# Attention and gated mixing in one kernel: first loads in halves, batch 0 in other banks, the last pair by subtiles, five chunks of q norms off TensorE, and a new set of planning numbers

## The chip, the cores and the metric

The kernel runs on one core of a Trainium2 chip. The metric is the device time of one execution in microseconds (us). Runs come as a median with their lowest and highest. A ratio is the mean time of one kernel's fast runs over the mean of the other's fast runs of the same rounds, with a 95% interval, so it is not quite the ratio of the medians quoted beside it. A run is called slow when it took over 1.5% longer than the fastest of its kernel. In the profiles PE is TensorE (PEld: its weight loads), DVE VectorE, ACT ScalarE, POOL GpSimd and SP SyncE; a q after the name marks the engine's issuing of transfers. The granted clock is TensorE's clock as a share of full speed.

## The reference, cut to what matters

```python
# q, k, v: 4 x 6336 x 256, float32
qn = q / (norm(q, axis=1) + 1e-06);  kn = k / (norm(k, axis=1) + 1e-06)
a = softmax(kn.transpose(0, 2, 1) @ qn / tau)       # 4 x 256 x 256
x = (v @ a).reshape(25344, 256)
H = maximum(x @ w_h, 0);  T = sigmoid(x @ w_t + b_t)
out = T * H + (1 - T) * x                           # float32
```

## The kernel before

Each batch has two stages. Stage one accumulates k.q and the squares over 50 subtiles of rows, 48 of 128 and two of 96 ("statistics"). A chain follows: norms, a broadcast of them (`cqb`), two exponentials, their transposes (`eps`), and weights folded with the attention matrix (`mr`). Stage two takes the rows of v in 25 pairs of subtiles: three products (`t`, `h`, `d`), a tanh and a relu on ScalarE, and two operations on VectorE, of which the second writes the result `o`. Four pairs fill one chunk of 1 MB, which SyncE stores to memory. A batch has six chunks and a tail pair. Stage one of batch b+1 is mixed into stage two of batch b.

A planner inside the program orders all of this when the program is built: it takes tasks with priorities, durations and buffers, and writes out one fixed order for each engine. So a changed duration or priority can move instructions anywhere.

Result chunks live in a ring of buffers, and stores are held back, so that they do not compete with the loads too early:

```python
O_BUFS = 7
LAG = 5
...
    def hold(b, j):                       # SyncE reads one row of a result
        nc.sync.dma_start(out=held_row, in_=og[(b, j)][0:1, 0, :])

    def plan_holds():
        for x, b, j in chunk_stores:      # x: the store of chunk b * NJ + j
            n = b * NJ + j + LAG
            y, g = begun.get(n, (None, 1e9))
            ...                           # late chunks are not held
            x.key = g + 1.6
            plan.add("SP", g + 1.5, 0.1, 0, [y], lambda n=n: hold(n // NJ, n % NJ), size=1024)
```

The tiny read `held_row` stands ahead of the store in SyncE's order, and it needs the first result of chunk n+LAG. So the store of chunk n is issued once chunk n+5 has begun, and its buffer is needed when chunk n+7 begins.

Places that the change touches:

```python
    for j in range(1, NJ - 1):            # first loads, in order of issue
        plan_load("q", 0, j);  plan_load("k", 0, j)
    ...                                   # tail; chunk 5 in quarters
    plan_load("q", 1, 0);  plan_load("k", 1, 0)
    ...                                   # w_h, w_t, then the bias
    plan_load("v", 0, 0)
...
    sg_t[b] = [new(f"sg{c}", [P, 512], f32, f"sg{c}_{b}") for c in range(2)]
...
    gs = act(copy_g, 0.58, 0.7, [dk], drop=[(first, "sg0"), (first, "sg1")])
```

## Time and profile before

| | before |
|---|---|
| median of 3 runs | 273.9 us (273.01 to 275.34) |
| span of the profiled run, its mean granted clock | 271.6 us, 0.985 |
| first product / last `d` group / last store issued | 48.47 / 263.51 / 265.88 us |

The list of DMA issues (size, then median us from issue to landing) says what it needs:

```profile
out_dram<-o SPq DMA_DIRECT2D x23, 1024.0 KB, 9.1
```

19.6 us for a transfer of about 9: nothing waits, and in the costliest groups VectorE's results have only 1.9 us of idle time before all 96 of them.

### The profile page before, as it was taken

How to read it: one execution, taken by the hardware profiler on the slowest of the kernel's cores; microseconds unless marked ns; L12 is line 12 of the kernel's file. 1: busy time of each engine (PE TensorE's matmuls, PEld its weight loads, DVE VectorE, ACT ScalarE, POOL GpSimd, SP SyncE). 2: the span in 40 equal slices, each digit the busy share in tenths (PEclk: the TensorE clock that was granted, in tenths of full speed). 3: DMA queues.
4: the chain of work that ended last, by engine and by line, in shares of the span. 5: the costliest groups of instructions: out<-in, count | busy, mean ns of one | idle time of the engine just before them, and what ended most of it. 6: DMA issues, size and time to landing. Idle time of an engine off the chain costs nothing.

```text
span 271.6 us, 6265 instructions
## 1 busy us (share of the span) xinstructions
PE 247.0 (91%) x2447; PEld 218.6 (80%) x2447; DVE 177.8 (65%) x366; ACT 191.5 (71%) x361; POOL 115.3 (42%) x153
## 2 busy tenths in 40 slices
PE   0697859999999999999999999999999999999980
PEld 0596757798999988999999888999998778878870
DVE  1000033658757897778777886767766888999991
ACT  1000034868969888889897888887875989988970
POOL 7221668596691095566928167775002110000000
PEclk9999997999999999999999999999999999999996
DMA  6999999999999999999999999999999999999996
GB/s 109 212 216 214 199 208 214 214 213 215 215 211 215 212 214 219 284 233 279 289 277 255 257 289 233 270 255 275 268 288 272 330 320 316 203 345 279 283 417 241
DMA packets 28430, 68.29 MB, mean 251 GB/s; under 512 B 13168, under 2 KB 15856, under 8 KB 25456
## 3 DMA queue, kind: packets, MB, share of 16 engines
q0 software_dynamic: 13184, 39.20, 73.6%
q1 hardware_dynamic: 15216, 28.69, 30.5%
q8 instruction: 19, 0.31, 0.4%
q14 instruction: 11, 0.09, 0.1%
HBM read 78.38 MB, written 25.95 MB: 384 GB/s over the span
## 4 chain that ended last, share of the span: by engine, by line
PE 76%; DMA 13%; DVE 4%; ACT 2%; issue 2%; POOL 1%; DVEq 0%; ACTq 0%; POOLq 0%
PE d L778 15%; PE h L778 15%; PE t L778 15%; DMA k<-in_k_dram 13%; PE sg L432 12%; PE sg L433 6%; PE vtps L738 6%; PE sg L435 2%; PE ah L667 1%; DVE pp L839 1%; PE t L809 1%; DVE o L858 1%; ACT d L818 1%; ACT uu L832 1%; PE eps L657 1%
## 5 line engine op out<-in xcount | busy, mean ns | idle before, releaser
L778 PEld LDWEIGHTS <-vtsb 128*128 128x128 f16 (+1 forms) x948 | 90.0, 99 | 13.4 <-issue 3.0
L432 PE MATMUL sg<-q,k 128*128 128x256 f16 x384 | 85.7, 278 | 15.2 <-DMA k<-in_k_dram 15.1
L839 DVE SCALAR_TENSOR_TENSOR pp<-uu,d 128x512 f32<-128x512 f32 (+1 forms) x100 | 67.7, 683 | 25.0 <-PE d L778 14.8
L433 PE MATMUL sg<-k 128*128 128x128 f16 x384 | 78.8, 224 | 0.0
L832 ACT ACTIVATE uu<-t 128x512 f32<-128x512 f32 (+1 forms) x100 | 59.5, 599 | 18.6 <-PE t L778 17.2
L858 DVE SCALAR_TENSOR_TENSOR o<-h,pp 128x512 f32<-128x512 f32 x96 | 65.3, 687 | 1.9
L818 ACT ACTIVATE d<-h 128x512 f32<-128x512 f32 (+1 forms) x100 | 57.8, 585 | 5.3 <-PE h L778 4.0
L432 PEld LDWEIGHTS <-k 128*128 128x128 f16 x384 | 38.5, 100 | 18.6 <-DMA k<-in_k_dram 15.9
L450 ACT ACTIVATE sq<-q 128x1024 f32<-128x1024 f16 x24 | 25.0, 1052 | 36.0 <-DMA q<-in_q_dram 36.0
L778 PE MATMUL t<-mr,vtsb 128*128 128x256 f16 x316 | 47.2, 272 | 0.4 <-ACT t L513 0.3
L778 PE MATMUL d<-mr,vtsb 128*128 128x256 f16 x316 | 46.5, 272 | 0.3 <-ACT d L818 0.2
L778 PE MATMUL h<-mr,vtsb 128*128 128x256 f16 x316 | 46.5, 272 | 0.3 <-DVE ri L635 0.3
L435 PE MATMUL sg<-q 128*128 128x128 f16 x192 | 42.8, 223 | 0.0
L433 PEld LDWEIGHTS <-k 128*128 128x128 f16 x384 | 38.3, 100 | 1.5 <-issue 0.3
L456 POOL TENSOR_TENSOR sq<-sq,sq 128x1024 f32<-128x1024 f32 x12 | 28.4, 2368 | 22.3 <-ACT sq L450 22.3
L513 ACT COPY t<-bias_all 128x512 f32<-128x512 f32 (+1 forms) x61 | 36.1, 592 | 1.3
L738 PE MATMUL vtps<-ident,v 128*128 128x128 f32 x144 | 27.9, 275 | 0.5 <-DVE vtsb L515 0.5
L549 DVE SCALAR_TENSOR_TENSOR junk<-sg,ident 128x128 f32<-128x128 f32 x16 | 4.6, 288 | 36.1 <-PE sg L435 35.5
L778 PEld LDWEIGHTS <-vT 128*128 128x128 f16 x240 | 23.4, 98 | 4.5 <-issue 0.5
L311 POOL DMA_DIRECT2D v<-in_v_dram x24 | 13.3, 555 | 31.1 <-PE vtps L738 21.9
L515 DVE COPY vtsb<-vtps 128x256 f32<-128x256 f32 (+2 forms) x42 | 17.6, 419 | 10.0 <-PE vtps L738 9.9
L311 POOL DMA_DIRECT2D q<-in_q_dram x27 | 15.1, 558 | 16.0 <-DMA q<-in_q_dram 8.9
(77 smaller groups left out, 252.1 us busy)
## 6 DMA issues: line engine op xcount, KB each, us to landing
out_dram<-o SPq DMA_DIRECT2D x23, 1024.0 KB, 9.1
v<-in_v_dram POOLq DMA_DIRECT2D x24, 512.0 KB, 18.1
q<-in_q_dram POOLq DMA_DIRECT2D x23, 512.0 KB, 16.7
k<-in_k_dram POOLq DMA_DIRECT2D x23, 512.0 KB, 17.6
out_dram<-o SPq DMA_DIRECT2D x2, 512.0 KB, 6.3
out_dram<-ot SPq DMA_DIRECT2D x4, 192.0 KB, 5.8
q<-in_q_dram POOLq DMA_DIRECT2D x4, 128.0 KB, 8.6
k<-in_k_dram POOLq DMA_DIRECT2D x4, 128.0 KB, 6.6
```

The lines of the kernel that those rows point to most:

```text
L311: nc.gpsimd.dma_start(out=t[:, s : s + n, :], in_=main_rows(src)[:, j * CH + s : j * CH + s + n, :])
L432: nc.tensor.matmul(sg[c][:, 0:C], kc, qa, start=first, stop=False)
L433: nc.tensor.matmul(sg[c][:, C : C + P], kc, kc, start=False, stop=False)
L435: nc.tensor.matmul(sg[c][:, C + P : C + 2 * P], qa[:, cs], qa[:, cs], start=False, stop=last)
L456: add(out=sq, in0=sq, in1=other)
L513: nc.scalar.copy(out=out, in_=in_)
L738: nc.tensor.transpose(ps[:, u, 0:nr], v.bitcast(f32), ident0[0:nr, 0:nr])
L778: nc.tensor.matmul(out[0:nr, u, :], vt[u][kt][:, 0:nr], mr[kt][:, col * C : (col + 1) * C], **flags(u, kt))
L818: nc.scalar.activation(out=d[0:nr, :, :], in_=ps_t["h", b, i][0:nr, :, :], func=Act.Relu, scale=0.5)
L832: nc.scalar.activation(out=uu[0:nr, :, :], in_=ps_t.pop(("t", b, i))[0:nr, :, :], func=Act.Tanh, scale=-0.5)
L839: nc.vector.scalar_tensor_tensor(out=pp[0:nr, :, :], in0=el.pop(("uu", b, i))[0:nr, :, :], scalar=1.0, in1=ps_t.pop(("d", b, i))[0:nr, :, ...
L858: nc.vector.scalar_tensor_tensor(out=ot, in0=ps_t.pop(("h", b, i))[0:nr, :, :], scalar=0.0, in1=el.pop(("pp", b, i))[0:nr, :, :], op0=AluO ...
```

## The change

Its intent: begin the products of batch 0 earlier, shorten the end, take q norms of a fifth chunk off TensorE, and retune the planner's numbers for the new shape. The diff, cut to its core:

```diff
-LAG = 5
-UNTIL = 65
-AHEAD = 15
-BY_DMA = 1
-MOVE = 150e3
-APART = 4
-V_AHEAD = -2
+LAG = 6
+UNTIL = 61
+AHEAD = 20
+BY_DMA = 3
+MOVE = 165e3
+APART = 5
+V_AHEAD = 0
 PRIO = {  # ... twelve pairs of priorities, all other values
-ENDS = [17.5, 46, 64.5]
+ENDS = [24.5, 46, 68.5]
 ...
-    for j in range(1, NJ - 1):
+    b_ld = [ ... load_b(u) ... ]          # the bias now right after chunk 0
+    for j in range(1, NJ - 2):
 ...
+    for n, j in ((2, NJ - 2), (1, NJ), (4, NJ - 1)):
+        for part in range(n):
+            plan_load("q", 0, j, n, part); plan_load("k", 0, j, n, part)
-    plan_load("q", 1, 0)
-    plan_load("k", 1, 0)
+    plan_load("q", 1, 0, 2, 0)            # halves
+    plan_load("k", 1, 0, 2, 0)
     w_ld = [ ... ]
-    plan_load("v", 0, 0)
+    plan_load("v", 0, 0, 2, 0)
+    plan_load("q", 1, 0, 2, 1); plan_load("k", 1, 0, 2, 1); plan_load("v", 0, 0, 2, 1)
 ...
+    def sg_tag(b, c):
+        return f"sg{c}" if b else "h"     # batch 0 in the banks of h
 ...
+            halves = [slice(0, 1), slice(1, 2)] if g == NP * B - 1 else [slice(0, 2)]
 ...                                       # product and result once per half
```

The cut leaves out `HEAD` and `TAIL` (6 to 4, 63 to 67), a fixed order of the relus with each tanh behind its relu, the transposes of batch 0's exponentials in a bank of `h`, and two finer rules of the planner.

## The prediction

> **What bounds the kernel now.** I read the views from coarse to fine: the page's busy shares and its slices, then the stretches, then every instruction around the end of the first batch's statistics and around the end of the kernel. The page first.
>
> ```profile
> PE 247.0 (91%) x2447; PEld 218.6 (80%) x2447; DVE 177.8 (65%) x366; ACT 191.5 (71%) x361; POOL 115.3 (42%) x153
> ...
> PE   0697859999999999999999999999999999999980
> ...
> GB/s 109 212 216 214 199 208 214 214 213 215 215 211 215 212 214 219 284 233 279 289 277 255 257 289 233 270 255 275 268 288 272 330 320 316 203 345 279 283 417 241
> ```
>
> TensorE is the fullest engine, and its only thin slices are the first six (to about 41 us) and the last. The reader should not trust 91% alone, because overlapping matmuls count as busy. So I took the step from one start to the next: a group of four 256-column matmuls starts 0.44 us after the one before it (109 ns each), and a 128-column one takes 56 ns. Pricing every matmul in TensorE's order at these steps (0.22 us for 512 columns, for a pair of float32 transposes and about that for the float32 broadcast) gives 236.8 us of work. From the first product at 48.47 us, 209.4 us of it are left, and the last group of TensorE ends at about 263.9: 215.5 us in all. So after 48.5 us only some 6 us (3%) are not work, about 1 us of it in each of the stretches around the later chains. Before 48.5 us the loss is far larger. Three stretches, whose columns are the length, busy time and count of PE, PEld, DVE, ACT and POOL, the granted clock, the DMA share and GB/s:
>
> ```profile
> 37.50:41.00 3.50, 0.48 (x6) 0.45 (x6) 2.08 (x14) 2.54 (x4) 1.93 (x3) 1.00 1.21 203
> 41.00:45.00 4.00, 4.00 (x22) 2.63 (x22) 2.00 (x8) 1.09 (x4) 3.00 (x6) 0.57 1.07 214
> 45.00:48.50 3.50, 2.98 (x28) 2.18 (x26) 0.85 (x2) 2.83 (x5) 3.47 (x4) 1.00 1.05 210
> ```
>
> TensorE idles, then runs 22 matmuls in 4 us at a clock of 0.57, then waits again. The timeline around it (start, length, what, idle before and its releaser):
>
> ```profile
> 29.35 0.28 PE L432 MATMUL sg<-q,k 128*128 128x256 f16 x1 [1.15 <-DMA k<-in_k_dram]
> ...
> 37.29 0.22 PE L435 MATMUL sg<-q 128*128 128x128 f16 x1
> 40.53 0.28 PE L432 MATMUL sg<-q,k 128*128 128x256 f16 x1 [3.02 <-DMA k<-in_k_dram]
> ...
> 40.88 0.65 PE L608 MATMUL cqb<-dcat,ones 128*128 128x256 f32 x2
> ...
> 44.41 0.63 PE L657 MATMUL eps<-ident,e 128*128 128x128 f32 x2
> ...
> 48.47 0.60 PE L778 MATMUL t<-mr,vtsb 128*128 128x256 f16 x4
> ```
>
> The first batch's statistics end at 37.29; its chain (norms, softmax, folded weights) lets the first product go at 48.47. In these 11.2 us TensorE does 5.3 us of priced work (8 subtiles of batch 1, the bias presets, the chain's own matmuls), so 5.9 us are lost. ACT shows one reason:
>
> ```profile
> 38.06 2.00 ACT L450 ACTIVATE sq<-q 128x1024 f32<-128x1024 f16 x2 [36.04 <-DMA q<-in_q_dram]
> 39.97 0.63 ACT L600 COPY gs<-sg 128x256 f32<-128x256 f32 x2
> ```
>
> The copy that frees the two statistics banks sits behind two squares of batch 1 and ends at 40.6; batch 1 takes the same banks, so its first matmul could not have run earlier even with its data there. The named releaser, k, landed at almost the same moment (40.48). Both hold it, and the change must remove both. Then the order puts six subtiles and three 512-column presets, at the low clock, in front of the transposes at 44.41, though the first exponential was done at 42.60.
>
> **What the Trainium skill says.** "TensorE: Matmul & The Clock Gate", section "Back-to-back issue gap", gives N/2.4 + 2.5 ns: 109 ns for 256 columns. The trace agrees (0.44 us for four), so there is nothing to win per matmul. The same page, Part 1 on the clock gate, says that TensorE drops to half rate after an idle window of about 3.4 us. The trace shows a clock of 0.57 just after 3.0 us of idling, so a gap somewhat under the stated window was enough here. "DMA: Bandwidth & Descriptors", section "Where 436 GB/s comes from", puts the ceiling at 435 GB/s. In this trace q, then k of batch 1, 1 MB each as read, land at 38.06 and 40.48, which is 2.4 us for each, 433 GB/s: the loads at the start are at the ceiling, so only their order can help. "Perfetto Trace Analysis", section "DMA Optimizations", says that smaller pieces can let some work start sooner where the DMA engines are idle; here they aren't, yet the point still applies to the first use of a chunk.
>
> **The change part by part.** I read the order of both kernels on each engine and priced it with the rows above.
>
> (a) Chunk 4 of batch 0 in halves. TensorE waited 1.15 us at 29.35 for the whole of k. From the 24.4 us at which chunk 3 landed, 26 subtiles at 0.444 us would end at 35.97; the first half of chunk 4 lands at about 26.9, before chunk 3 is used up at 27.98, and the last quarter of chunk 5 at about 35.6 plus 0.9 us of its own work. So the statistics end near 36.5 against 37.5: 1.0 us.
>
> (b) The bias spreading (three 512-column matmuls, 0.65 us) moves into the DMA waits before 24 us, where it is free.
>
> (c) Batch 0 accumulates in the banks of h, and the first pieces of batch 1's q and k are halves: these land at 36.9 and 38.1, and nothing waits for the bank copy. Four subtiles of batch 1 (1.3 us) run from 38.1. DVE needs from 37.33 to 39.76 in the trace, 2.4 us, to get from the statistics to the diagonal factors, so those are ready at 38.9. The broadcast has three subtiles ahead of it and goes at about 39.1 instead of 40.88. From the broadcast to the end of both exponentials the trace has 2.2 us (to the first one 1.7), so 41.3 (40.8).
>
> (d) The order then has v transposes, both exponential transposes and both folds, back to back, with no presets and only one subtile. The first v transpose stands ahead of the exponentials and needs the first half of v: q half, k half, two weights of 0.25 MB and v half are 2 MB, as much as q and k before, so it lands at the same 40.5. Transposes to 41.6; evacuations (0.37 us each) and folds (0.44 us each) to 42.8; the two ACT evacuations of the folds (1.45 us for two) to 43.7. First product at about 44.0 instead of 48.47: 4.5 us earlier.
>
> (e) What is left then. Five chunks' q norms off TensorE remove 3 x 8 x 2 = 48 matmuls of 128 columns (2.7 us); two bias rows go (0.4 us); two more chunks of batch 3 transposed on TensorE instead of by DMA add 32 transposes (1.8 us). The whole order comes to 235.4 us, 1.3 us less. But less filler ran during the chain: 26.05 us are done by the first product against 27.37. The rest is 209.4 us in both. So (e) pays only for the filler that (d) left out, and the 4.5 us stand for both.
>
> (f) ACT now does the two squares of batch 1 after the folds (2.0 us), ahead of the first relu and the first tanh. One t bank, so the second t waits: tanh ends near 47.5, the preset near 48.0. I count two holes of some 0.6 us against 0.3 before: +0.8.
>
> (g) TensorE is thinly loaded from 36.5 to 44. If the clock falls as at 41 us, half rate over one such stretch of 3.4 us costs up to 1.7 us, now when the products are due. With a chance of one in four: +0.4.
>
> (h) The last pair. In the kernel before:
>
> ```profile
> 263.51 0.60 PE L778 MATMUL d<-mr,vT_t 128*96 128x256 f16 x4
> 263.71 0.59 ACT L832 ACTIVATE uu<-t 96x512 f32<-96x512 f32 x1 [0.39 <-PE t L778]
> ...
> 264.46 0.67 DVE L839 SCALAR_TENSOR_TENSOR pp<-uu,d 96x512 f32<-96x512 f32 x1
> 265.17 0.69 DVE L858 SCALAR_TENSOR_TENSOR ot<-h,pp 96x512 f32<-96x512 f32 x1
> 265.88 0.33 SPq L870 DMA_DIRECT2D out_dram<-ot  x1
> ```
>
> Two DVE operations become four of half width, each perhaps 0.42 us (my estimate from 412 ns for a 256-column operation in the costliest groups), 1.7 us instead of 1.4, and the tanh, not the d product, gates the first of them. I expect no gain from this part: +0.5.
>
> (i) The other tuned numbers spread the statistics of batches 1 to 3 over 24.5, 21.5 and 22.5 pairs instead of 17.5, 28.5 and 18.5, and leave more TensorE work between the end of the statistics and the broadcast (5.5, 7.3 and 9.1 us against 4.0, 3.4 and 3.9). That should take most of the roughly 1 us lost at each later chain, though ACT gets 6 more squares (6.3 us): -0.8.
>
> Sum: -4.5 + 0.8 + 0.4 + 0.5 - 0.8 = -3.6 us; 273.9 - 3.6 = 270.3 us.
>
> **The rivals.** First, the chain stays behind its own latency or v: TensorE's order is fixed, and a v half that lands 1.5 us late, behind the small weight pieces, holds the exponentials too. Then the first product comes at 45.5, and the time is about 271.8. Against it: the DMA rate stayed between 199 and 216 GB/s written in the early slices, pieces of 128 KB included. Second, ACT or DVE becomes the bound: per pair ACT and DVE together have about 3.9 us in the evenly spread stage, 1.97 us each, against some 2.2 us of TensorE; this stretch is the tightest, and a stall of 2% there (60 us) is 1.2 us, which with (f) at its worst makes 272. For it: tanh waits and product waits already add to 17 and 15 us. Against it: the old stage with 28.5 pairs was as tight (2.2 us per pair) and shows TensorE at its steps. Third, the better case: no clock drop, no boundary loss and the tail neutral, so that the whole 4.5 us and another 1.5 stand: 268.
>
> **Range and chances.** The 4.5 us are the firm part (plus or minus 1), the other terms add about 1.5 us either way, and the three times of before spread over 2.3 us. That makes 267.6 to 272.8 for 8 in 10. Faster by over 2% needs 268.4, only the better case: 0.23. Slower by over 2% needs a new stall of 9 us: 0.03. Within 2%: 0.74.
>
> **What would show it.** The wait of 1.15 us at chunk 4 is gone and the statistics end near 36.5; batch 1 starts near 38.1; the broadcast runs near 39.1; the first product near 44.0 (47 or later makes (d) wrong); a clock below 0.7 between 40 and 48 makes (g) real. From the first product to TensorE's last group it should be about 216 us again; more than 219 means rival two. From the last d group's start to the last store's issue took 2.37 us; more in the new kernel confirms (h). If the time is under 268, I have missed idle time in the steady stage.

## More of the kernel before

SyncE's own timeline (start, length, what), from the profile before:

```profile
103.90 0.62 SPq L897 DMA_DIRECT2D held_row<-o  x1
104.58 0.67 SPq L872 DMA_DIRECT2D out_dram<-o  x1
115.14 0.35 SPq L870 DMA_DIRECT2D out_dram<-ot  x1
115.73 0.51 SPq L897 DMA_DIRECT2D held_row<-o  x1
116.29 0.58 SPq L872 DMA_DIRECT2D out_dram<-o  x1
124.93 0.51 SPq L897 DMA_DIRECT2D held_row<-o  x1
```

VectorE's results around the same time:

```profile
103.19 0.68 DVE L858 SCALAR_TENSOR_TENSOR o<-h,pp 128x512 f32<-128x512 f32 x1
...
115.03 0.68 DVE L858 SCALAR_TENSOR_TENSOR o<-h,pp 128x512 f32<-128x512 f32 x1
...
124.21 0.69 DVE L858 SCALAR_TENSOR_TENSOR o<-h,pp 128x512 f32<-128x512 f32 x1
```

Each hold starts right as a chunk's first result ends. The result at 103.19 opens chunk 5 and lets the store of chunk 0 go at 104.58. Chunk 6 begins at 115.03 and chunk 7, which takes chunk 0's buffer, at 124.21. The store has 19.6 us.

## The result, and the profile after

| | before | after |
|---|---|---|
| median | 274.33 us (273.01 to 275.34, 4 runs) | 283.25 us (282.62 to 286.89, 4 runs) |
| ratio of the fast runs | | 1.0325 (1.0275 to 1.0376) |

The change made the kernel 3.3% slower, outside the predicted range. The profiled run of the changed kernel was slow (286.89 us; its fast runs took 282.62 to 283.6). So I ran it again unaltered (first experiment below) and read that profile, of a fast run of 282.78 us with a span of 281.0 us. The page's slices of TensorE and its clock, from that run:

```profile
PE   0786977899999989989888899997979999999990
...
PEclk9999999999999999999999999999999999999996
```

Where before had solid nines from the seventh slice on, there are now eights and sevens between the fifteenth and the thirtieth of 40, with the clock at 90% or more in every slice but the last. The chain that ended last, as shares of the span by line:

```profile
DMA out_dram<-o 21%; DMA k<-in_k_dram 14%; PE t L791 10%; PE h L791 9%; PE d L791 9%; PE sg L445 6%; PE sg L446 3%; PE vtps L751 3%; DVE o L872 2%; ACT uu L844 2%; ACT t L526 2%; ACT d L831 1%; PE t L822 1%; DVE pp L852 1%; SPq L911 1%
```

Before, the only DMA in that row was the load of k (13%). Now the stores of the result lead it. Two of the costliest groups (count, busy time and mean ns, then idle time just before them and its main releaser), from the same page:

```profile
L872 DVE SCALAR_TENSOR_TENSOR o<-h,pp 128x512 f32<-128x512 f32 x96 | 65.7, 687 | 11.8 <-DMA out_dram<-o 7.8
...
L791 PE MATMUL h<-mr,vtsb 128*128 128x256 f16 (+1 forms) x348 | 51.5, 272 | 8.4 <-DVE o L872 8.4
```

VectorE waits for a store before it writes a result; that keeps a bank of `h` occupied, and TensorE waits for the bank. One such place, on SyncE, VectorE and TensorE:

```profile
114.68 0.61 SPq L911 DMA_DIRECT2D held_row<-o  x1
115.34 0.57 SPq L886 DMA_DIRECT2D out_dram<-o  x1
```

```profile
113.96 0.69 DVE L872 SCALAR_TENSOR_TENSOR o<-h,pp 128x512 f32<-128x512 f32 x1
...
116.34 0.68 DVE L872 SCALAR_TENSOR_TENSOR o<-h,pp 128x512 f32<-128x512 f32 x1
...
118.80 0.68 DVE L872 SCALAR_TENSOR_TENSOR o<-h,pp 128x512 f32<-128x512 f32 x1
...
121.42 0.68 DVE L872 SCALAR_TENSOR_TENSOR o<-h,pp 128x512 f32<-128x512 f32 x1
...
124.95 0.69 DVE L872 SCALAR_TENSOR_TENSOR o<-h,pp 128x512 f32<-128x512 f32 x1 [1.28 <-DMA out_dram<-o]
```

```profile
125.70 0.60 PE L791 MATMUL h<-mr,vtsb 128*128 128x256 f16 x4 [1.15 <-DVE o L872]
```

The result at 113.96 opens chunk 6 and releases the store of chunk 0, issued at 115.34. Four pairs later, at 124.95, chunk 7 wants its buffer. That is 9.6 us, and the store has only just landed. With LAG 6 of seven buffers, each store has one chunk of work to land in, instead of two. In this trace six first results of a chunk wait so, for 1.28, 1.48, 2.01, 1.15, 1.93 and 2.48 us (the trace names the store for the first five and nothing for the last), and TensorE stands idle before `h` for 1.15, 1.34, 1.91, 0.84, 1.41 and 1.79 us, together 8.4 us.

"Perfetto Trace Analysis", section "Optimization Strategy", of the Trainium skill says that the same gap repeating on the engine that should be saturated can mean too few buffers. The trace agrees in part: four of the six gaps follow each other about 11 us apart, but the count of buffers is that of before; what changed is how late each is given back.

The front did move. TensorE's rows in the fast run:

```profile
39.94 0.28 PE L445 MATMUL sg<-q,k 128*128 128x256 f16 x1 [1.46 <-DMA k<-in_k_dram]
...
40.95 0.65 PE L622 MATMUL cqb<-dcat,ones 128*128 128x256 f32 x2
...
45.45 0.27 PE L791 MATMUL t<-mr,vtsb 128*128 128x256 f16 x1
```

The first product comes at 45.45, 3.0 us earlier than before. In the slow run, the first profile, the half of k landed later, as TensorE's row shows:

```profile
41.44 0.39 PE L445 MATMUL sg<-q,k 128*128 128x256 f16 x1 [3.00 <-DMA k<-in_k_dram]
```

The clock fell. Two stretches of that run (length, busy time and count of PE, PEld, DVE, ACT and POOL, granted clock, DMA share, GB/s):

```profile
41.00:45.00 4.00, 3.56 (x18) 2.52 (x18) 0.39 (x2) 0.00 (x0) 3.71 (x7) 0.50 1.07 170
45.00:50.00 5.00, 4.34 (x15) 2.14 (x14) 1.94 (x9) 3.40 (x9) 1.58 (x3) 0.50 1.08 208
```

The clock is 0.50 where the chain needs TensorE, and the first product came at 49.38, 3.9 us later than in the fast run; the time is 4.1 us longer. (The clock of the slow run fell once more, from 152.78 to 156.19 us, among the waits for stores.) This is no part of the 3.3%, which compares fast runs.

### The profile page after: what moved, and what is told of

The parts are those of the page before. It is cut to its first block, busy times and chain, and to the rows that moved or that the text cites. A ratio compares the mean times of both kernels' runs of the same rounds, so it can differ in the third digit from the quotient of the medians.

```text
span 285.1 us, 6233 instructions
## 1 busy us (share of the span) xinstructions
PE 251.9 (88%) x2429; PEld 218.8 (77%) x2429; DVE 180.0 (63%) x378; ACT 200.8 (70%) x367; POOL 132.9 (47%) x170
## 4 chain that ended last, share of the span: by engine, by line
PE 50%; DMA 28%; ACT 9%; DVE 4%; issue 3%; POOL 2%; SPq 1%; DVEq 0%; ACTq 0%; POOLq 0%
DMA out_dram<-o 17%; PE t L791 12%; DMA k<-in_k_dram 11%; PE h L791 10%; PE d L791 9%; PE sg L445 7%; PE vtps L751 4%; PE sg L446 3%; ACT uu L844 3%; ACT t L526 2%; DVE o L872 2%; ACT d L831 2%; PE ah L681 2%; ACT sq L463 1%; PE t L822 1%
## 5 line engine op out<-in xcount | busy, mean ns | idle before, releaser
L791 PEld LDWEIGHTS <-vtsb 128*128 128x128 f16 (+1 forms) x1044 | 100.0, 99 | 27.4 <-issue 14.5
L852 DVE SCALAR_TENSOR_TENSOR pp<-uu,d 128x512 f32<-128x512 f32 (+2 forms) x101 | 68.6, 679 | 32.2 <-ACT uu L844 22.2
L872 DVE SCALAR_TENSOR_TENSOR o<-h,pp 128x512 f32<-128x512 f32 x96 | 65.6, 686 | 10.3 <-DMA out_dram<-o 6.3
L791 PE MATMUL h<-mr,vtsb 128*128 128x256 f16 (+1 forms) x348 | 51.7, 273 | 7.3 <-DVE o L872 7.3
L469 POOL TENSOR_TENSOR sq<-sq,sq 128x1024 f32<-128x1024 f32 x15 | 35.4, 2360 | 48.6 <-ACT sq L463 48.6
L791 PE MATMUL t<-mr,vtsb 128*128 128x256 f16 (+1 forms) x348 | 52.9, 274 | 3.1 <-ACT t L526 2.0
L791 PE MATMUL d<-mr,vtsb 128*128 128x256 f16 (+1 forms) x348 | 52.6, 274 | 0.0
L526 ACT COPY t<-bias_all 128x512 f32<-128x512 f32 (+1 forms) x66 | 39.1, 592 | 1.9
L448 PE MATMUL sg<-q 128*128 128x128 f16 x144 | 32.4, 225 | 0.0
L463 ACT ACTIVATE sq<-q 128x1024 f32<-128x1024 f16 x30 | 31.2, 1048 | 0.0
L751 PEld LDWEIGHTS vtps<-ident,v 128*128 128x128 f32 x144 | 17.5, 144 | 2.7 <-issue 0.7
L472 POOL TENSOR_TENSOR sq<-sq 128x512 f32<-128x512 f32 x15 | 19.2, 1282 | 0.5
```

Of the source, the lines that this page charges most:

```text
L448: nc.tensor.matmul(sg[c][:, C + P : C + 2 * P], qa[:, cs], qa[:, cs], start=False, stop=last)
L463: nc.scalar.activation(out=sq, in_=qa, func=Act.Square)
L469: add(out=sq, in0=sq, in1=other)
L526: nc.scalar.copy(out=out, in_=in_)
L751: nc.tensor.transpose(ps[:, u, 0:nr], v.bitcast(f32), ident0[0:nr, 0:nr])
L791: nc.tensor.matmul(out[0:nr, u, :], vt[u][kt][:, 0:nr], mr[kt][:, col * C : (col + 1) * C], **flags(u, kt))
```

## The experiments

Two theories. Theory one (S in the expectations): the store is released one chunk too late for its buffer (LAG 6 of 7), which costs about 10 us, and the rest of the change is roughly neutral. Its rival (F): the new order (priorities, more work on ScalarE and VectorE) starves TensorE, and the store waits only fill gaps that would be there anyhow. The experiments on the front and the end then size the prediction's own terms. In the names, "o8" means the changed kernel with eight result buffers.

Where I give "lost" time between two milestones on TensorE, it is the time between them less the work there, priced as in the prediction.

**1. The changed kernel, unaltered.**

> The changed kernel unaltered, as the yardstick on this chip: 283 us. Its first profile fell in the slow state; here I want one in the fast state. If the profile shows VectorE waiting for stores of the o tiles again (four or five waits of about 2 us) and the first product near 48 us instead of the 44.0 that I predicted, both theories have their evidence: theory S (stores: a store is released one chunk later than before, LAG 6 of 7 o buffers instead of 5, so VectorE finds no free o tile, the h bank stays taken and TensorE stops; 6 to 8 us) and theory F (front: the first chain came no earlier because the small early loads are slower, and the tuned priorities leave holes later; the stores are only where the delay shows).

282.9 us (282.58 to 286.01, 4 runs), ratio 1.0361 (1.0298 to 1.0424). Its profile is the one read above; the first product came at 45.45 there, earlier than the 48 that I had expected.

**2. Eight result buffers.** The order on every engine is unaltered; only the ring is longer.

```diff
-O_BUFS = 7
+O_BUFS = 8
```

> One more o buffer (8 instead of 7), every engine's order unchanged row by row. Theory S: the waits of VectorE for stores vanish and so do TensorE's holes of 2 us after d products; 6 to 8 us less, about 276 us. Theory F: 282 to 283.5 us, at most 1 us gained.

273.02 us (272.59 to 274.07, 4 runs), ratio 0.998 (0.9942 to 1.0018): 9.9 us less than the unaltered kernel on the same chip. The group of results in its page:

```profile
L872 DVE SCALAR_TENSOR_TENSOR o<-h,pp 128x512 f32<-128x512 f32 x96 | 65.6, 686 | 1.4
```

The idle time before the results fell from 11.8 to 1.4 us, and TensorE no longer waits for `o` at all. The stores still take 10.0 us from issue to landing. The gain of 9.9 us is more than the 6 to 8 that I had expected. Theory one explains the whole slowdown. Its rival falls: same order, same work, no slowdown.

**3. Release a chunk sooner, with seven buffers.** Only what SyncE reads changes.

```diff
-lambda n=n: hold(n // NJ, n % NJ)
+lambda n=n: hold((n - 1) // NJ, (n - 1) % NJ)
```

> The small read that holds each store back waits for the first result of the chunk before, so each store goes one chunk (four pairs) earlier, as in the kernel before; seven o buffers, orders of TensorE, VectorE, ScalarE and GpSimd unchanged. Theory S: about 276 us again, within 1 us of the run with eight buffers. Theory F: 282 to 284. A third possibility: the earlier stores take bandwidth from the loads and some of the gain goes, 278 to 280.

275.83 us (275.45 to 278.17, 5 runs), ratio 1.007 (1.0032 to 1.0108). Releasing the store sooner takes back 7 of the 10 us without any further memory. Its profile (the 278.17 us run, with the clock drop at the front) still has one wait of 1.7 us for a store, at 190.58. So eight buffers do better by 2.8 us, where I had expected less than 1; one wait accounts for part of that, and I did not find the rest.

**4. The kernel before, with six buffers.** The planner still counts seven, so all orders are those of before; only the slack shrinks to one chunk.

```diff
-        plan.ring(tag, bufs)
+        plan.ring(tag, O_BUFS if tag == "o" else bufs)   # and "o": 6 in nbuf
```

> The kernel before with six o buffers instead of seven and its plan untouched, so every engine's order is the same; the slack between the release of a store and the need of its buffer becomes one chunk, as in the changed kernel. Theory S: VectorE waits for stores appear, and it is slower than before by 5 to 9 us (279 to 283). Theory F: within 1.5 us of before.

286.27 us (284.55 to 288.92, 4 runs, the longest slow and not in the ratio), ratio 1.0438 (1.0379 to 1.0496). The waits (us in total, times, longest) on VectorE and TensorE:

```profile
DVE o L858 <- DMA out_dram<-o: 9.1, 4, 3.1
```

```profile
PE h L778 <- DVE o L858: 7.6, 4, 2.7
```

The same slack of one chunk, made in the kernel before with nothing else of the change, gives the same waits and a loss of 12 us, more than the 5 to 9 that I had expected. The waits are 9.1 us of it; the trace also shows the clock at 0.50 for 3.41 us right after the second of these waits (140.49 to 143.91). The rest I did not take apart.

**5. The kernel before, with eight buffers.** The control in the other direction.

```diff
-O_BUFS = 7
+O_BUFS = 8
```

> The kernel before with eight output buffers instead of seven, every instruction in the same order. The theory that a store needs about 9 us and the kernel before gives it two chunks of work (about 20 us) says that a third chunk buys nothing: ratio 1.000 within 0.5%, no wait of VectorE for an output transfer in either. If stores hold up the kernel before as well, it gains 1 us or more.

274.24 us (272.62 to 275.14, 4 runs), ratio 0.9973 (0.9926 to 1.002): the same, as expected. Two chunks of slack are enough, one is not.

**6. The old planning numbers in the changed kernel.** All constants, priorities and ends of before (LAG 5 with them).

```diff
-LAG = 6    # and AHEAD, BY_DMA, MOVE, APART, V_AHEAD, PRIO, HEAD, TAIL, ENDS
+LAG = 5    # all as before
```

> The changed program (loads in halves, batch 0 in the banks of h, bias early, relu and tanh in a fixed order, last pair in halves) with every tuned number of the kernel before (store lag 5, priorities, spread of the statistics, four chunks of q norms, transposes by DMA from chunk 1). With eight o buffers the changed kernel begins its products 3.9 us earlier than before but ends level. Theory C (the new tuned numbers cost 3 us in the later chains and the start-up): this version keeps the early start and loses nothing later, 269.5 to 271. Theory P (the new program itself, its ACT order and its 2 us of squares after the first chain, costs it): 272.5 to 274.

280.84 us (279.82 to 281.84, 4 runs), ratio 1.0235 (1.0201 to 1.0269). Both theories missed: I had expected the store waits to go and the rest to be about as good as before. The store waits do go, but the planner makes another order out of the old numbers: the first product comes at 47.63, 4.8 us are lost from there to the second broadcast (before: 1.4) and 5.4 from the last broadcast to the last `d` (before: 2.0). The clock also fell, from 42.19 to 49.02 us. The old numbers fitted the old program; putting them back is no test of LAG alone, and it tells nothing against theory one.

**7. The same with five chunks apart.**

```diff
-APART = 4
+APART = 5
```

> As the version with all the old tuned numbers, but five chunks of q norms off TensorE instead of four. By the count this takes 48 matmuls of 56 ns, 2.7 us, from TensorE and gives ScalarE six squares. If TensorE is the bound throughout: 2 to 2.7 us faster than with four chunks. If ScalarE is nearly as tight, as my second rival said: within 1 us of it.

282.19 us (281.88 to 282.51, 4 runs), ratio 1.0285 (1.0262 to 1.0308). The first product comes at 44.82, but 6.3, 3.5, 4.8 and 5.7 us are lost in the four stretches after it. That is 1.35 us slower than with four chunks, outside both expectations. Again an order that nobody tuned.

**8. o8, last pair whole.** Only the last operations on VectorE differ.

```diff
-            halves = [slice(0, 1), slice(1, 2)] if g == NP * B - 1 else [slice(0, 2)]
+            halves = [slice(0, 2)]
```

> The changed kernel with eight o buffers, the last pair whole again; only VectorE's last six instructions differ. My prediction had the halves as a cost of 0.5 us: then this is 0.3 to 0.7 us faster than the same with halves (273.0). If the halves help as the change intends, it is 0.3 us or more slower.

272.89 us (272.6 to 273.64, 6 runs), ratio 0.9951 (0.9932 to 0.997), against 273.02 with halves (run 2, other rounds). The end with halves (run 2), then whole:

```profile
264.27 0.60 PE L791 MATMUL d<-mr,vT_t 128*96 128x256 f16 x4 [0.23 <-ACT d L831]
...
265.92 0.41 DVE L872 SCALAR_TENSOR_TENSOR ot<-h,pp 96x256 f32<-96x256 f32 x1
266.25 0.41 DVE L852 SCALAR_TENSOR_TENSOR pp<-uu,d 96x256 f32<-96x256 f32 x1
266.69 0.42 DVE L872 SCALAR_TENSOR_TENSOR ot<-h,pp 96x256 f32<-96x256 f32 x1
267.14 0.33 SPq L884 DMA_DIRECT2D out_dram<-ot  x1
```

```profile
265.05 0.60 PE L791 MATMUL d<-mr,vT_t 128*96 128x256 f16 x4 [0.23 <-ACT d L831]
...
266.26 0.67 DVE L852 SCALAR_TENSOR_TENSOR pp<-uu,d 96x512 f32<-96x512 f32 x1
266.97 0.69 DVE L872 SCALAR_TENSOR_TENSOR ot<-h,pp 96x512 f32<-96x512 f32 x1
267.68 0.33 SPq L884 DMA_DIRECT2D out_dram<-ot  x1
```

From the last `d` to the last store's issue: 2.87 us in halves, 2.63 whole, 2.37 before. So halving costs 0.24 us on this path, the new order of the end another 0.26, and the time of the kernel does not resolve it.

**9. o8, the old loads at the front,** with batch 0 still in the banks of `h`.

```diff
-    for n, j in ((2, NJ - 2), (1, NJ), (4, NJ - 1)):
+    for n, j in ((1, NJ - 2), (1, NJ), (4, NJ - 1)):
-    plan_load("q", 1, 0, 2, 0); plan_load("k", 1, 0, 2, 0)   # ... v, second halves
+    plan_load("q", 1, 0); plan_load("k", 1, 0)               # ... bias, then v
```

> The changed kernel with eight o buffers, but the early loads in their old sizes and order (whole chunks, bias loads late); batch 0 still in the banks of h. If the halves are what brings the first product forward, it comes at 47 us or later again and the time is 275 to 277. If the banks alone do it, the first product stays near 45 and the time within 1 us of 273.0.

283.89 us (283.47 to 284.64, 4 runs), ratio 1.035 (1.0324 to 1.0376). The first product came at 49.0, but the planner also made a worse order of everything after: 4.3, 5.7 and 5.6 us lost in the stretches up to the fourth broadcast, against 4.4, 2.1 and 2.3 in run 2. The time is far outside both expectations. Mostly it measures the new order; hence the next.

**10. o8, each pair of halves issued as one load.** The planner still plans halves, so the orders on TensorE, VectorE and ScalarE stay; only the transfers differ.

```diff
+            if parts == 2:
+                x.fn = (lambda nm=nm, b=b, j=j: load(nm, b, j, 0, CH)) if s == 0 else None
```

> The changed kernel with eight output buffers, and with each pair of half loads (q, k and v of the first chunks of batch 1, chunks 4 and 5 of batch 0) issued as one whole load where its first half stood. The order of instructions on TensorE, VectorE and ScalarE is unaltered; only the transfers differ. If the halves are what lets batch 1 start early, the statistics of batch 0 end about 1 us later than the 37.4 to 38.3 us seen with halves, batch 1 starts at 40 us or later, TensorE idles about 3 us before it, the clock drops, and the first product comes at 47 us or later instead of 44.6 to 46.2: 275 to 277 us. If the halves do nothing and the banks of h alone did it, the first product stays below 46.5 and the time within 1 us of the 273.0 us of the kernel with eight buffers.

277.33 us (276.12 to 277.89, 4 runs), ratio 1.01 (1.006 to 1.0139): 4.3 us slower than run 2. TensorE's rows around the end of batch 0's statistics:

```profile
38.31 0.22 PE L451 MATMUL sg<-q 128*128 128x128 f16 x1
41.46 0.40 PE L448 MATMUL sg<-q,k 128*128 128x256 f16 x1 [2.93 <-DMA k<-in_k_dram]
```

Run 2, the same place:

```profile
37.40 0.22 PE L448 MATMUL sg<-q 128*128 128x128 f16 x1
39.09 0.28 PE L445 MATMUL sg<-q,k 128*128 128x256 f16 x1 [1.48 <-DMA k<-in_k_dram]
```

In this pair of traces whole loads start batch 1 2.4 us later; the clock falls to 0.50, and the first product comes at 49.40 instead of 44.61. (The statistics end 0.9 us later, but that shows nothing: with halves and the same order on TensorE, the last matmul of the statistics starts anywhere from 36.85 to 38.37 us in seven profiles.) The four times, 276.12 and more, lie clear of run 2's 274.07 and less, so the early front needs the halves; the banks of `h` alone do not give it. Whether the halves alone would, without the banks, was not tried. Nor are the halves enough in every run: the slow run above and the profile of run 3 have them and the same late front (49.38 and 49.09), with the clock at 0.50 in both. So most of the 4.8 us goes with the clock.

**11. o8, the bias tile cleared first on VectorE.** Only VectorE's first six instructions change places; the copy of the identity, which waits for GpSimd, also goes from second to last.

```diff
+        nc.vector.memset(btb, 0.0)
         make_identity(nc, ident0)
-        nc.vector.tensor_copy(out=ident, in_=ident0)
         ...                               # ones, row
-        nc.vector.memset(btb, 0.0)
         nc.vector.memset(half, 0.5)
+        nc.vector.tensor_copy(out=ident, in_=ident0)
```

> The changed kernel with eight output buffers, and with the clearing of the bias tile moved from fifth to first place on VectorE, so that GpSimd need not wait 1.28 us for it before it issues its first loads. Only the first six instructions of VectorE change places. If that wait is what makes the transfers thin at 8 to 12 us and delays the statistics, they end 0.5 to 1 us sooner (36.6 to 37.4), batch 1 starts sooner, the clock drops in fewer runs, and the time is 272.0 to 272.8. If the transfers catch up anyway, the time is 273.0 within 0.5.

273.05 us (271.74 to 273.73, 4 runs), ratio 0.9944 (0.9903 to 0.9984). GpSimd's first issue of the bias, in run 2 and then here:

```profile
4.31 1.00 POOL L294 DMA_DIRECT2D btb<-in_moe_b_t_dram  x2 [1.29 <-DVE half L286]
```

```profile
2.98 1.00 POOL L294 DMA_DIRECT2D btb<-in_moe_b_t_dram  x2
```

The stretch from 8 to 12 us, in run 2 and then here:

```profile
8.00:12.00 4.00, 3.17 (x22) 2.68 (x23) 0.00 (x0) 0.00 (x0) 1.60 (x3) 1.00 0.98 160
```

```profile
8.00:12.00 4.00, 3.12 (x22) 2.69 (x23) 0.00 (x0) 0.00 (x0) 1.96 (x4) 1.00 1.07 211
```

The wait and the thin transfers (160 GB/s against 211) are gone, yet nothing came of it: the statistics ended at 38.15, later than hoped, batch 1 started at 38.94 and the first product came at 44.95. It is the miss that I had allowed for: the loads catch up, or lose it again, later; from 37 to 41 us they moved 153 GB/s here and 181 in run 2.

**12. o8, the bias tile first, and the first of two squares of batch 1 before the chain.** The expectation speaks of two squares; the edit moves one of them, as ScalarE's rows below show.

```diff
+            if b == 0:
+                squares(1, 0, 0)          # the first half, right after the copy of the statistics
                                           # (and not at their old place)
```

> The changed kernel with eight output buffers, the clearing of the bias tile first, and the first two squares of batch 1 on ScalarE directly after the copy of the statistics, in its idle time before the exponentials, instead of after the chain. If those squares (2 us) are what makes the second t wait 0.6 us near 50 us, the work lost from the first product to the second broadcast shrinks from 4.4 us to 3.5 or less, and the time is 271.5 to 272.3, below both kernels. If the squares now delay the exponentials (their q half lands at 39 to 41 us), the first product moves back by up to 1 us and the time is 273 or more.

272.9 us (272.12 to 273.87, 6 runs), ratio 0.9945 (0.9913 to 0.9978). In run 2 TensorE waited twice for the preset of `t`:

```profile
49.30 0.60 PE L791 MATMUL t<-mr,vtsb 128*128 128x256 f16 x4 [0.43 <-ACT t L526]
51.26 0.60 PE L791 MATMUL t<-mr,vtsb 128*128 128x256 f16 x4 [0.44 <-ACT t L526]
```

Here one square of 1.06 us goes ahead of the exponentials and one of 1.05 us stays behind the chain; both waits for the preset are gone, and one for a result has come:

```profile
38.61 1.06 ACT L463 ACTIVATE sq<-q 128x1024 f32<-128x1024 f16 x1
...
45.78 1.05 ACT L463 ACTIVATE sq<-q 128x1024 f32<-128x1024 f16 x1
```

```profile
50.86 0.60 PE L793 MATMUL h<-mr,vtsb 128*128 128x256 f16 x4 [0.48 <-DVE o L874]
```

From the first product to the second broadcast 3.7 us are lost instead of 4.4, but the first product comes at 45.24 instead of 44.61. In run 8, where both squares stay and both waits for the preset are there, the same stretch lost 3.6 us. So moving one square removes those two waits; that it shortens the stretch is not shown, and the time didn't move.

Runs 8, 11 and 12 beat the kernel before by 0.5%, each with an interval that leaves 1 out. Run 2 has the same time but does not clear its own before. I can't rank the four.

## Why the prediction was wrong

The step that failed is (i), "The other tuned numbers". It priced the numbers as a group, by what they do to the statistics and to TensorE's filler, at -0.8 us, and never looked at LAG 5 to 6 against seven result buffers. The runs put +9.9 us there (282.9 with seven buffers, 273.02 with eight; releasing each store a chunk sooner, in run 3, takes back 7.1). It could have been seen blind: before, a store needs 9.1 us to land and a chunk takes 9 to 12 us (holds at 103.90, 115.73 and 124.93), so going from two chunks of slack to one leaves none. The prediction even wrote that slower by 2% "needs a new stall of 9 us", and gave it 0.03 because no part of its list could make one; the list had left a line of the diff out.

The other steps, with eight buffers (run 2) against before, so that LAG is out of the way:

- (a), (c), (d) The first product came at 44.61, against 44.0 predicted and 48.47 before: 3.9 of the 4.5 us. For (c) and (d) the mechanism held: run 10 shows that the halves are needed. But (a) brought nothing: the 1.15 us wait at chunk 4 is gone, yet the statistics end at 37.6, not 36.5, and before at 37.5. Batch 1 starts at 39.09 rather than 38.1, and the broadcast (40.10 against 39.1) and the first product inherit it. Part of the gain was not in the prediction's sum: all three profiles of the order of before (with seven, six and eight buffers) show the clock at 0.50 for 3.41 us, beginning at 41.5 to 41.9, and run 2 shows no such fall. In the profile before, those 3.41 us held 1.8 us of priced work, so up to 1.6 us (an estimate) is the clock, which the prediction counted only as a risk of the new kernel; that much of the agreement is luck. In the other profiles of the changed order without that fall the first product came at 44.95 to 46.17.
- (b) The presets themselves are free. Loading the bias early costs GpSimd 1.29 us, which the prediction missed, but run 11, without that wait, is no faster beyond the noise.
- (e) The work that was equal in price stays equal: from the first product to the start of the last `d` both orders have 208.9 us of it.
- (f) Predicted +0.8; the start-up, from the first product to the second broadcast, lost 3.0 us more than before (4.42 against 1.45). The two holes that (f) counted are there, 0.43 and 0.44 us, and moving one of ScalarE's squares removes them (run 12). The rest of the loss (in all 2.2 us more than before in run 8, 3.0 in run 2) is other short waits for ScalarE and one for a load, which I did not take apart.
- (g) The clock drop is real: the trace of the slow run shows it, and 2 of the 9 runs of the unaltered changed kernel took 286 us or more at the lowest clocks of the nine (0.971 and 0.976). It cost 4.1 us there and 2.4 in run 3 (278.17 against a mean of 275.7 for its other runs), not 1.7: in both traces it lasted 10.24 us, through the whole chain, and not 3.4.
- (h) The end took 0.5 us longer, just as predicted, but only half of it is due to the halves (run 8). Something else hid it: the kernel ended 4.1 us after the last store's issue (267.14 to 271.2) and before 5.7 us (265.88 to 271.6). The last store landed 2.2 us after its issue, before 4.7. In the last stretches before, then in run 2, the transfers are fuller before (GB/s is the last number):

```profile
265.00:268.00 3.00, 0.00 (x0) 0.00 (x0) 0.82 (x2) 0.00 (x0) 0.00 (x0) 0.80 1.02 416
```

```profile
265.00:268.00 3.00, 0.00 (x0) 0.00 (x0) 2.08 (x5) 0.00 (x0) 0.00 (x0) 0.87 0.42 168
```

- (i), apart from LAG: predicted -0.8; the three later stretches lost 1.6 us more than before (2.06 + 2.30 + 1.93 against 1.56 + 1.12 + 1.97). The sign was wrong.

The sum for run 2: -3.9 (front) + 3.0 (start-up) + 1.6 (later stretches) + 0.5 (end) - 1.7 (from the last store's issue to the end) = -0.5 us; the spans are 271.2 and 271.6. So the front's gain was given back inside the kernel, and 9.9 us of store waits came on top. Even without them the time is above the 270.3 us predicted, (f) first of all.

Two citations of the prediction, on the rate of loads and on the step of a matmul, leave out what else those sections say; the last list has it. That the loads at the start were at their limit rests on the busy share of the DMA engines, 1.05 to 1.21 in the prediction's three stretches.

The test in the prediction, "more than 219 means rival two", was too coarse. To the start of the last `d` it read 228.6 us in the unaltered kernel and 219.7 with eight buffers, against 215.0 before, so it fired; but the first excess is VectorE standing still for a store, not VectorE or ScalarE being full. A sum of time does not tell an engine that works from one that waits.

## What to carry to other kernels

Where a kernel both rings its buffers and delays the release of its stores, compare two numbers: buffers minus delay, in time of work, and the landing time of a store under load. Go through a list of retuned constants one by one with that question, for a single digit there can outweigh everything else in the change. And to test one constant of a planned program, hold the order fixed, as with one buffer more here; putting old constants back makes a new program.

## What the Trainium skill lacked or had wrong

- "TensorE: Matmul & The Clock Gate", Part 1, gives an idle window of about 3.4 us for the drop to half rate, and calls the window free-running. The traces agree with the window: in all fourteen the clock changes only at whole multiples of 3.41 us after its first rise, and the falls before the end last 3.41, 6.83 or 10.24 us. But the window need not be idle: in the 3.41 us before each of the 14 falls TensorE had priced work for 8 to 42% of the time, and some windows with 34% or more were followed by none. So the length of one gap does not tell: 1.92 us of idling (up to 24.36 us, run 4) was followed by a fall and 2.73 us (run 12) was not.
- "DMA: Bandwidth & Descriptors", section "Where 436 GB/s comes from", which the prediction quotes for 435 GB/s, gives that for the on-chip side and says that for transfers from memory the memory's side, about 358, binds. Here, with one core running, two loads went at 433 GB/s, counted as read.
- "TensorE: Matmul & The Clock Gate", section "Back-to-back issue gap", gives the formula that the prediction quotes for a matmul by itself, and about 81 ns for 128 columns in a stream with weight loads. Here such a stream (before, 2447 weight loads for 2447 matmuls) steps at 56 ns.
- "Perfetto Trace Analysis", "Optimization Strategy", names the count of buffers for repeating gaps. No page that I read says that a held-back store has the same effect at an unchanged count: 9.9 us here, from one chunk of slack against a landing time of 9.5 us.
- No page that I read gives the landing time of a large store beside a stream of loads. Here 1 MB took 9.1 to 10.3 us in the median, with an issue that mostly lasted 0.6 us.
